# Chunked attention and two feed-forward layers on one core: weight conversion moved to the end of each attention tick with a fourth tile, v in another row order, relu squared from PSUM

## The chip, the cores and the metric

One core of a Trainium2 chip runs the whole program. The metric is device time in microseconds. The kernel before took 1264.05 us, the median of three runs (1263.99 to 1264.7).

## The reference

Attention is computed within chunks of 64 positions: 4 batches, 8 heads, 576 positions (9 chunks) and 64 numbers a head. Its output becomes x, 2304 tokens by 512, and goes through two layers.

```
scores = scale * (q_c @ k_c.T);  attn = softmax(scores);  x = attn @ v_c
h = max(x @ w_in, 0);            x = (h * h) @ w_out                    # 512 -> 2048 -> 512
for e in range(4): out += p[:, e] * (max(x @ w1[e], 0) @ w2[e])         # 512 -> 1024 -> 512
```

The first layer's weights arrive as 64-bit floats; q, k, v and the rest are 32-bit.

## The kernel before

**Ticks.** The order of all instructions is the order of the code; each engine works through its own list in that order and waits where an operand is missing. The first part runs in ticks r = 0, 1, 2, ... (the loop at L660). A tick of attention treats one tile of 128 positions (two chunks, all 8 heads), 18 tiles in all: `s1_stage(r)` makes the scores on TensorE and subtracts the row maximum on VectorE (two reduces L239 and two subtracts L240); `norm_stage(r-1)` divides by the row sums (L251 to L254, VectorE); `s2_stage(r-2)` transposes the weights (L260) and ScalarE copies them out (L262); `s0_stage(r+1)` transposes the next q and then the next k (L218, copies L222); `s3_stage(r-2)` multiplies by v (L274) and writes x as a rounded part (L281, ScalarE) and a rest (L282, VectorE); `exp_stage(r)` is ScalarE's exponential (L246). So `s3` stands on TensorE behind both transposes of tick r.

**First layer.** From tick 5 on, step m = r - 5 runs between these stages: `l1(m)` is one 128-row slice of x @ w_in for one block of tokens (384 or 512), 12 matmuls (L298), then relu (L308, ScalarE), the square (L309, VectorE), its rounded part (L311) and its rest (L312). `l2(m-1)` is 12 matmuls of the second product (L328), for the slice that the step before made. In a tick the first nine matmuls of `l1` come after `s1`, the last three after the q transpose, a quarter of `l2` (d = 0) before the k transpose, a quarter (d = 1) after it, then `s3`, and the last two quarters (d = 2, 3) at the tick's end.

**Weight units.** A unit is 128 rows or columns of w_in or w_out. Unit load (L108, L113) brings 512 KB into one of 4 `raw` tiles. `unit_convert` turns 64-bit into 32-bit in a `cv` tile: two operations on ScalarE (L125, L126), four on VectorE (L127, L130, L135, L138), two on GpSimd (L139, L140). `unit_split`, one tick or more later, makes a rounded part on ScalarE (L151) and a rest on GpSimd (L152), and so frees the `cv` tile. The first eight units are called u0 to u7 here, in the list `order`: w_in 0, w_in 1, w_out 0, w_in 2, w_out 1, w_in 3, w_out 2, w_out 3. They are converted in ticks 2, 3, 4, 4, 5, 6, 6, 7 (`FIRST`) and split at the end of the following tick, after that tick's conversions. `l1(m)` needs w_in m, from the start of tick 5 + m; `l2(m-1)` needs w_out m-1, from the middle of that tick. In the code before, L125 to L130 stand before the `s2` of a tick, and L135 to L140 before its `s3`.

**Loads.** SyncE issues the loads in the order of the code: in each tick first the weight units, then q and k of tile r + 2, and in some ticks v. A unit's load waits until a `raw` tile is free, and everything behind it on SyncE waits too. Eight semaphores tell of landed DMAs, taken in turn.

**PSUM.** From tick 5 on all the stages of attention share three banks ("t") in turn; `l1` has one bank ("h").

Of the kernel before, what the change touches and what calls it, by code (L numbers as in the profile page):

```python
# [10 lines left out]
F32 = mybir.dt.float32  # L11
F32R = mybir.dt.float32r
AF = mybir.ActivationFunctionType
ALU = mybir.AluOpType
# [4 lines left out]
P = 128  # L19
CH = 64  # L20
# [10 lines left out]
WARM = 8  # L31
SECOND = [-3, -2, -1, 1, 2, 3, 4, 5]
RAW_BUFS = 4
CV_BUFS = 3
HALF = 384
NSUP = 3
SWAP = 63
# [9 lines left out]
def tile_kernel(ctx, tc, q, k, v, moe_w_in, moe_w_out, moe2_p, moe2_w1, moe2_w2, out):  # L47
    nc = tc.nc
# [3 lines left out]
    E, _, F2 = moe2_w1.shape  # L52
    KD = DM // P
    HX = H // 2
    NTILE = NT // P
    NCB = S // CH
# [14 lines left out]
    staging = ExitStack()  # L71
    cvp = staging.enter_context(tc.tile_pool(name="cvp", bufs=CV_BUFS))
    rawp = staging.enter_context(tc.tile_pool(name="rawp", bufs=RAW_BUFS))
# [22 lines left out]
    def bank(tags):  # L96
        n = turn.get(tags, 0)
        turn[tags] = n + 1
        tag = tags[n % len(tags)]
        return ps.tile([P, 512], F32, tag=tag, name="ps" + tag, bufs=BUFS[tag])  # L100
# [58 lines left out]
    qkv, vt = {}, {}  # L159
    xh, xl = {}, {}  # L160
# [27 lines left out]
    def new_v(b):  # L188
        vt[b] = qkp.tile([P, HX, NCB, D], F32, tag="v", name="v")

    def load_v(b, c0, c1):
        if b not in vt:
            new_v(b)
        for h in range(H):
            j, x = divmod(h, 2)
            nc.sync.dma_start(
                out=vt[b][x * CH:(x + 1) * CH, j, c0:c1, :],
                in_=v[b, h, c0 * CH:c1 * CH, :].rearrange("(c k) d -> k c d", k=CH),
            )
            if h % 2:  # L200
                yield

    def load_v_chunk(b, c, engines):
        if b not in vt:
            new_v(b)
        for x in range(2):
            engines[x].dma_start(
                out=vt[b][x * CH:(x + 1) * CH, :, c, :],
                in_=v[b, x::2, c * CH:(c + 1) * CH, :].rearrange("j k d -> k j d"),
            )  # L210
            yield

# [12 lines left out]
    def s1_stage(t, tags):  # L225
        qt, kt = qT.pop(t), kT.pop(t)
        pt = [bank(tags)[:, :HX * CH].rearrange("p (j k) -> p j k", j=HX) for _ in range(2)]
        for c in range(2):
            cs = slice(c * CH, (c + 1) * CH)
            for j in range(HX):  # L230
                for x in range(2):
                    r = slice(x * CH, (x + 1) * CH)
                    nc.tensor.matmul(  # L233
                        pt[x][cs, j, :], lhsT=qt[r, j, cs], rhs=kt[r, j, cs], start=True, stop=True
                    )
        e = qkp.tile([P, HX, 2, CH], F32, tag="e", name="e", bufs=LAG_A + 1)
        mx = qkp.tile([P, 2, HX, 1], F32, tag="mx", name="mx")
        for x in range(2):
            nc.vector.tensor_reduce(out=mx[:, x], in_=pt[x], axis=AX.X, op=ALU.max)  # L239
            nc.vector.tensor_tensor(  # L240
                out=e[:, :, x, :], in0=pt[x], in1=mx[:, x].to_broadcast([P, HX, CH]), op=ALU.subtract
            )
        et[t] = e

    def exp_stage(t):
        nc.scalar.activation(out=et[t], in_=et[t], func=AF.Exp, scale=scale)  # L246
# [17 lines left out]

    def s3_stage(t, tags):
        a = aT.pop(t)
        pt = bank(tags).rearrange("p (j s) -> p j s", j=HX)
        for j in range(HX):
            for c in range(2):
                b, cc = divmod(2 * t + c, NCB)  # L270
                cs = slice(c * CH, (c + 1) * CH)
                for x in range(2):
                    r = slice(x * CH, (x + 1) * CH)
                    nc.tensor.matmul(  # L274
                        pt[r, j, cs], lhsT=vt[b][r, j, cc, :], rhs=a[r, j, cs], start=True, stop=True
                    )
        tb, off = block_of[t]
        if off == 0:
            new_x(tb)
        hi = xh[tb][:, :, off:off + P]  # L280
        nc.scalar.copy(hi, pt)  # L281
        nc.vector.tensor_tensor(  # L282
            out=xl[tb][:, :, off:off + P], in0=pt, in1=hi.bitcast(F32), op=ALU.subtract
        )


    steps = [(p, tb, f) for p in range(npass1) for tb in range(NB) for f in range(G)]
# [3 lines left out]
    def l1(i):  # L291
        p, tb, f = steps[i]
        T = BLOCKS[tb]
        ah, al = halves[p * G + f, 0]
        ph = bank("h" if "w" not in late else "httt")
        for kk in range(KD):
            for n, (w, x) in enumerate(((ah, xh), (ah, xl), (al, xh))):
                nc.tensor.matmul(  # L298
                    ph[:, :T], lhsT=w[:, kk, :], rhs=x[tb][:, kk, :],
                    start=(kk == 0 and n == 0), stop=(kk == KD - 1 and n == 2),  # L300
                )
            if kk < KD - 1:
                yield
        o = GP_AT + i % (LAG + 1) * 1024
        hi, lo = ar[:, o:o + 512], ar[:, o + 512:o + 1024]
        gh[i], gl[i] = hi, lo
        r = rp.tile([P, 512], F32, tag="r", name="r")
        nc.scalar.activation(out=r[:, :T], in_=ph[:, :T], func=AF.Relu)  # L308
        nc.vector.tensor_tensor(out=r[:, :T], in0=r[:, :T], in1=r[:, :T], op=ALU.mult)  # L309
        yield  # L310
        nc.scalar.copy(hi[:, :T], r[:, :T])  # L311
        nc.vector.tensor_tensor(  # L312
            out=lo[:, :T], in0=r[:, :T], in1=hi[:, :T].bitcast(F32), op=ALU.subtract
        )
# [46 lines left out]
    for sp in range(NSUP):  # L361
        if sp < NSUP - 1:
            r = [starts[2 * sp] + i * P for i in range(3)] + [starts[2 * sp + 1] + i * P for i in range(3)]
        else:
            r = [starts[NB - 1] + i * P for i in range(3)] + [starts[2 + i] + HALF for i in range(3)]
# [200 lines left out]
    def at(tick, kind, fn, *args):  # L566
        jobs[kind].setdefault(max(0, tick), []).append((fn, args))

    def do(tick, kind):
        return [fn(*args) for fn, args in jobs[kind].pop(tick, ())]  # L570

    for t in range(2, NTILE):
        at(t - 2, "load", load_qk, t, (nc.sync, nc.scalar if t == 2 else nc.sync))
    for b in range(B):
        if b == 0:
            for c in (2, 3):
# [22 lines left out]
    with tc.manual_schedule():  # L599
# [39 lines left out]
        def run(chunks, n=None):  # L639
            while n is None or n > 0:  # L640
                try:
                    next(chunks)
                except StopIteration:
                    return
                n = None if n is None else n - 1
# [13 lines left out]
        for r in range(LEAD + NS + LAG):  # L659
            m = r - LEAD  # L660
            tags = "ttthaaaa" if m < 0 else "t"
            ch = mlp(m) if m >= 0 else iter(())
            if r == NTILE + LAG_A:
                att.close()
                late["x"] = ctx.enter_context(tc.tile_pool(name="xq", bufs=1, side="right"))
                late["w"] = lw.enter_context(tc.tile_pool(name="wpb", bufs=RING_B, side="right"))
            merge(do(r, "load"))
            if r < NTILE + LAG_A:
                if r < NTILE:
                    s1_stage(r, tags)  # L670
                if 0 <= r - 1 < NTILE:
                    norm_stage(r - 1)
                conv = do(r, "convert")
                for c in conv:
                    next(c)
                run(ch, 3)
                if 0 <= r - LAG_A:
                    s2_stage(r - LAG_A, tags)
                if r + 1 < NTILE:
                    s0_stage(r + 1, tags, 0)  # L680
                run(ch, 2)
                if r + 1 < NTILE:
                    s0_stage(r + 1, tags, 1)
                for c in conv:
                    run(c)
                run(ch, 1)
                if 0 <= r - LAG_A:
                    s3_stage(r - LAG_A, tags)
                if r < NTILE:
                    exp_stage(r)  # L690
                do(r, "split")
            else:
                if r == SWAP:
                    staging.close()
                    late["raw"] = ctx.enter_context(tc.tile_pool(name="raw", bufs=1, reuse_waits="tile"))
                for fn, args in early.pop(r, ()):
                    fn(*args)
                if r > y0_at:
                    next(late.setdefault("y0", y_combine(0)), None)
                if m < NS:  # L700
                    run(ch, KD + 2)
                    conv = do(r, "convert")
                    for c in conv:
                        next(c)
                    run(ch, 1)
                    for c in conv:
                        run(c)
                    do(r, "split")
            if m < NS:
                run(ch)  # L710
# [68 lines left out]
```

## Time and profile before

| | |
|---|---|
| median of 3 runs | 1264.05 us |
| profiled execution, device time | 1261.85 us |
| its span, first to last instruction | 1260.1 us |
| TensorE matmul busy | 1231.7 us (98%), 7048 instructions |
| TensorE weight loads | 1090.4 us (87%) |
| VectorE | 705.0 us (56%), 1135 |
| ScalarE | 521.3 us (41%), 934 |
| GpSimd | 628.8 us (50%), 507 |
| granted TensorE clock, mean | 0.989 |

Busy shares are means over the span. The first part (attention and first layer, to about 500 us) and the second layer have different limits, so a share says little of a stage; the windows below cut it. Matmul busy time is modelled. In the profile PE is TensorE, PEld its weight loads, DVE VectorE, ACT ScalarE, POOL GpSimd, SP SyncE.

### The profile page before, as it was taken

To read this page: it belongs to the slowest core of one execution; us is meant where nothing else is said; L and a number is where in the kernel's file an instruction comes from. 1 tells how busy PE (TensorE), PEld (TensorE's weight loads), DVE (VectorE), ACT (ScalarE), POOL (GpSimd) and SP (SyncE) were. 2 spreads that over 40 slices of the span, in tenths; PEclk is the share of its full clock that TensorE was granted. 3 is DMA by queue.
4 is the path that set the end of the run, shared out by engine and by line. 5 is a ranking of instruction groups with operands and counts; after the bars stand their busy time and mean duration, and the time that the engine had idled before them with its cause. 6 is when DMAs were issued, how large, how long until landed. Compare 5 with 4: busy or idle time off the path is not lost.

```text
span 1260.1 us, 18090 instructions
## 1 busy us (share of the span) xinstructions
PE 1231.7 (98%) x7048; PEld 1090.4 (87%) x7048; DVE 705.0 (56%) x1135; ACT 521.3 (41%) x934; POOL 628.8 (50%) x507
## 2 busy tenths in 40 slices
PE   6799999999999999999999999999999999999998
PEld 5688788988988988888888888888888888888887
DVE  4876667755765355355555573555555735555555
ACT  3654455432432223633333355333333553333331
POOL 0530046431432022766776686767766866666650
PEclk7889999999999999999999999999999999999999
DMA  9947012210201000222222223222222232222211
GB/s 209 197 77 168 5 51 87 66 51 17 67 1 50 1 1 17 67 67 68 67 67 67 68 76 109 68 69 70 69 69 70 66 122 68 70 67 69 67 35 66
DMA packets 136838, 87.19 MB, mean 69 GB/s; under 512 B 62769, under 2 KB 120113, under 8 KB 136753
## 3 DMA queue, kind: packets, MB, share of 16 engines
q1 hardware_dynamic: 133088, 85.12, 24.9%
q10 hardware_dynamic: 3664, 0.92, 0.4%
q8 instruction: 55, 0.90, 0.3%
q14 instruction: 31, 0.25, 0.1%
HBM read 81.30 MB, written 4.72 MB: 68 GB/s over the span
## 4 chain that ended last, share of the span: by engine, by line
PE 91%; DVE 3%; ACT 1%; issue 0%; POOL 0%; DVEq 0%
PE psa L543 32%; PE pst L498 24%; PE psa L328 14%; PE pst L298 9%; PE psh L298 6%; PE psh L498 4%; PE pst L274 1%; PE pst L233 1%; PE pst L218 1%; DVE cv L127 0%; PE pst L260 0%; DVE r L309 0%; DVE cv L130 0%; DVE ar L312 0%; DVE cv L135 0%
## 5 line engine op out<-in xcount | busy, mean ns | idle before, releaser
L543 PE MATMUL psa<-ar 128*128 128x512 f32 x1728 | 445.7, 393 | 0.0
L543 PEld LDWEIGHTS psa<-ar 128*128 128x128 f32 x1728 | 320.0, 188 | 50.3
L466 POOL TENSOR_TENSOR ar<-raw,ar 128x896 fp32r<-128x896 f32 x96 | 204.2, 2129 | 274.4 <-ACT ar L465 274.4
L498 PE MATMUL pst<-ar 128*128 128x384 f32 x1728 | 339.2, 335 | 0.9 <-ACT u L507 0.9
L498 PEld LDWEIGHTS pst<-ar 128*128 128x128 f32 x1728 | 307.3, 188 | 22.8 <-ACT u L507 1.6
L556 DVE SCALAR_TENSOR_TENSOR o<-psa,prob,o 128x512 f32<-128x512 f32 x270 | 201.5, 747 | 173.4 <-PE psa L543 173.4
L139 POOL TENSOR_TENSOR raw<-raw 128x512 f32<-128x512 f32 x32 | 36.2, 1131 | 230.0 <-DVE raw L138 97.6
L456 POOL TENSOR_TENSOR raw<-raw 128x256 f32<-128x256 f32 x192 | 141.3, 754 | 8.8 <-DMA raw<-in_moe_w 5.2
L475 POOL TENSOR_TENSOR ar<-raw,ar 128x512 fp32r<-128x512 f32 x96 | 123.4, 1306 | 12.5 <-ACT ar L474 12.5
L309 DVE TENSOR_TENSOR r<-r 128x512 f32<-128x512 f32 (+1 forms) x80 | 64.9, 811 | 108.9 <-ACT r L308 108.8
L328 PE MATMUL psa<-ar 128*128 128x512 f32 (+1 forms) x480 | 114.7, 379 | 1.3 <-POOL ar L152 1.2
L507 ACT COPY u<-pst 128x384 f32<-128x384 f32 x96 | 46.0, 479 | 163.8 <-PE pst L498 163.8
L511 ACT ACTIVATE ar<-pst 128x384 fp32r<-128x384 f32 x96 | 47.2, 492 | 149.7 <-DVE pst L532 116.3
L328 PEld LDWEIGHTS psa<-ar 128*128 128x128 f32 x480 | 87.6, 191 | 14.3 <-POOL ar L152 1.5
L328 PE MATMUL psa<-ar,h 128*128 128x512 f32 (+1 forms) x320 | 93.7, 373 | 1.6 <-ACT ar L311 0.8
L511 ACT ACTIVATE ar<-psh 128x384 fp32r<-128x384 f32 x96 | 47.2, 492 | 109.8 <-DVE psh L521 78.6
L465 ACT CAST ar<-raw 128x896 fp32r<-128x896 f32 x96 | 90.1, 939 | 0.0
L312 DVE TENSOR_TENSOR ar<-r,ar 128x512 fp32r<-128x512 f32 (+1 forms) x80 | 61.6, 770 | 39.9 <-ACT ar L311 39.1
L512 DVE SCALAR_TENSOR_TENSOR ar<-psh,ar 128x384 fp32r<-128x384 f32 x96 | 53.5, 558 | 53.6 <-ACT ar L511 53.6
L311 ACT CAST ar<-r 128x512 fp32r<-128x512 f32 (+1 forms) x80 | 46.1, 577 | 71.0 <-DVE r L309 71.0
L512 DVE SCALAR_TENSOR_TENSOR ar<-pst,ar 128x384 fp32r<-128x384 f32 x96 | 53.5, 557 | 31.2 <-ACT ar L511 29.1
L298 PE MATMUL pst<-ar,h 128*128 128x512 f32 (+1 forms) x240 | 69.3, 370 | 0.0
(106 smaller groups left out, 1482.9 us busy)
## 6 DMA issues: line engine op xcount, KB each, us to landing
raw<-in_moe_w SPq DMA_DIRECT2D x48, 512.0 KB, 3.9
raw<-in_moe_w SPq DMA_DIRECT2D x48, 256.0 KB, 3.0
raw<-in_moe_w SPq DMA_DIRECT2D x96, 128.0 KB, 3.0
raw<-in_moe_w_in SPq DMA_DIRECT2D x16, 512.0 KB, 3.8
raw<-in_moe_w_out SPq DMA_DIRECT2D x16, 512.0 KB, 3.7
out<-o SPq DMA_DIRECT2D x18, 256.0 KB, 3.2
q<-in_q SPq DMA_DIRECT2D x16, 256.0 KB, 4.7
v<-in_v SPq DMA_DIRECT2D x24, 144.0 KB, 4.5
```

The source lines that it names most:

```text
L298: nc.tensor.matmul(ph[:, :T], lhsT=w[:, kk, :], rhs=x[tb][:, kk, :], start=(kk == 0 and n == 0), stop=(kk == KD - 1 and n == 2),)
L309: nc.vector.tensor_tensor(out=r[:, :T], in0=r[:, :T], in1=r[:, :T], op=ALU.mult)
L328: nc.tensor.matmul(o, lhsT=w, rhs=y, start=(f == 0 and n == 0), stop=(f == G - 1 and n == 2))
L456: nc.gpsimd.tensor_tensor(out=r[:, o], in0=r[:, a], in1=r[:, b], op=op)
L465: nc.scalar.copy(h, a)
L466: nc.gpsimd.tensor_tensor(out=l, in0=a, in1=h.bitcast(F32), op=ALU.subtract)
L475: nc.gpsimd.tensor_tensor(out=l, in0=a, in1=h.bitcast(F32), op=ALU.subtract)
L498: nc.tensor.matmul(p, lhsT=w[:, kk, :], rhs=y[:, kk, :], start=(kk == 0 and z == 0 and u in (0, 1, 3)), stop=(kk == 1 and z == 2 and u in ...
L511: nc.scalar.activation(out=h, in_=p, func=AF.Relu)
L512: nc.vector.scalar_tensor_tensor(out=l, in0=p, scalar=0.0, in1=h.bitcast(F32), op0=ALU.max, op1=ALU.subtract)
L543: nc.tensor.matmul(p, lhsT=w[:, ts], rhs=y[:, i, :], start=(i == 0 and z == 0), stop=(i == 1 and z == 2))
L556: nc.vector.scalar_tensor_tensor(out=o, in0=p, scalar=pe, in1=o, op0=ALU.mult, op1=ALU.add)
```

## The change

Four things change. `unit_convert` runs whole at the end of a tick of attention, after `exp_stage` and before the splits, with four `cv` tiles for three. The v tile holds, for odd j, the two heads of a pair in swapped row halves; `s1` writes the scores in that order, and `s3` runs the 32 matmuls one column half after the other, with alternating row halves, into two PSUM banks, which are read by two L281 and two L282 operations of half the size. The first chunks of v are loaded by four DMAs of 32 KB for two of 64 KB. The square becomes max(PSUM, 0) times the relu, and k of tile 2 is loaded from SyncE's queue, no longer from ScalarE's.

```diff
-CV_BUFS = 3
+CV_BUFS = 4
 def load_v(b, c0, c1):
             j, x = divmod(h, 2)
+            x ^= j % 2
 def load_v_chunk(b, c, engines):
-        for x in range(2):
+        vb = v[b].rearrange("(jj z) s d -> z s jj d", jj=2)
+        for z, x in ((0, 0), (1, 1), (3, 0), (2, 1)):
             engines[x].dma_start(
-                out=vt[b][x * CH:(x + 1) * CH, :, c, :],
-                in_=v[b, x::2, c * CH:(c + 1) * CH, :].rearrange("j k d -> k j d"),
+                out=vt[b][x * CH:(x + 1) * CH, z // 2::2, c, :], in_=vb[z, c * CH:(c + 1) * CH],
             )
 def s1_stage(t, tags):
             nc.vector.tensor_tensor(
-                out=e[:, :, x, :], in0=pt[x], in1=mx[:, x].to_broadcast([P, HX, CH]), op=ALU.subtract
+                out=e.rearrange("p (jj jb) x k -> p jj (jb x) k", jb=2)[:, :, slice(1, 3) if x else slice(0, 4, 3), :],
+                ...
 def s3_stage(t, tags):
-        pt = bank(tags).rearrange("p (j s) -> p j s", j=HX)
-        for j in range(HX):
-            for c in range(2):
-                ...
-                for x in range(2):
-                    r = slice(x * CH, (x + 1) * CH)
-                    nc.tensor.matmul(pt[r, j, cs], lhsT=vt[b][r, j, cc, :], rhs=a[r, j, cs], ...)
+        pt = [bank(tags)[:, :2 * P].rearrange("p (j s) -> p j s", j=2) for _ in range(2)]
+        for x in (1, 0):
+            for jj in range(HX // 2):
+                for c in range(2):
+                    ...
+                    for jb in range(2):
+                        j = 2 * jj + jb
+                        r = slice((x ^ jb) * CH, (x ^ jb) * CH + CH)
+                        nc.tensor.matmul(pt[jb][x * CH:(x + 1) * CH, jj, cs], lhsT=vt[b][r, j, cc, :], rhs=a[r, j, cs], ...)
-        nc.scalar.copy(hi, pt)
-        nc.vector.tensor_tensor(out=xl[tb][:, :, off:off + P], in0=pt, ...)
+        for jb in range(2):
+            hi = xh[tb][:, jb::2, off:off + P]
+            nc.scalar.copy(hi, pt[jb])
+            nc.vector.tensor_tensor(out=xl[tb][:, jb::2, off:off + P], in0=pt[jb], ...)
 def l1(i):
-        nc.vector.tensor_tensor(out=r[:, :T], in0=r[:, :T], in1=r[:, :T], op=ALU.mult)
+        nc.vector.scalar_tensor_tensor(out=r[:, :T], in0=ph[:, :T], scalar=0.0, in1=r[:, :T], op0=ALU.max, op1=ALU.mult)
-        at(t - 2, "load", load_qk, t, (nc.sync, nc.scalar if t == 2 else nc.sync))
+        at(t - 2, "load", load_qk, t)
 # the loop over ticks, r < NTILE + LAG_A
-                conv = do(r, "convert")
-                for c in conv:
-                    next(c)
                 run(ch, 3)
                 ...
-                for c in conv:
-                    run(c)
                 run(ch, 1)
                 ...  # s3_stage, exp_stage
+                for c in do(r, "convert"):
+                    run(c)
                 do(r, "split")
```

## Rows read from the trace of the kernel before

**Rows 1.** Windows: busy us and instructions of each engine; granted clock, DMA share.

```profile
20.00:40.00 20.00, 12.82 (x222) 11.37 (x224) 17.60 (x41) 11.83 (x22) 6.25 (x6) 0.84 1.08 205
40.00:60.00 20.00, 15.59 (x175) 13.91 (x172) 17.46 (x34) 11.99 (x24) 11.03 (x9) 0.85 0.87 198
80.00:100.00 20.00, 20.00 (x260) 18.03 (x257) 13.32 (x28) 10.91 (x22) 1.28 (x1) 1.00 0.33 76
```

**Rows 2.** Chain that ended last, 0 to 180 us: start, length, what.

```profile
74.94 1.49 PE psh L298 x7
...
93.82 0.54 PE psa L328 x3
94.36 0.44 PE pst L218 x4
...
95.32 1.08 PE pst L274 x32
96.40 1.27 PE psa L328 x6
97.67 0.91 PE pst L233 x30
```

**Rows 3.** Waits, 0 to 100 us: total, times, longest.

```profile
ACT cv L125 <- POOL ar L152: 14.4, 4, 6.1
```

**Rows 4.** Timeline of POOL, 17 to 76 us: start, length, operation.

```profile
52.85 2.84 POOL L152 TENSOR_TENSOR ar<-cv,ar 128x512 fp32r<-128x512 f32 x2
...
65.55 1.27 POOL L152 TENSOR_TENSOR ar<-cv,ar 128x512 fp32r<-128x512 f32 x1
71.23 1.04 POOL L139 TENSOR_TENSOR raw<-raw 128x512 f32<-128x512 f32 x1 [4.41 <-issue]
...
73.60 2.85 POOL L152 TENSOR_TENSOR ar<-cv,ar 128x512 fp32r<-128x512 f32 x2
```

**Rows 5.** Timeline of ACT, the same stretch.

```profile
39.30 0.59 ACT L281 CAST ar<-psh 128x512 fp32r<-128x512 f32 x1 [0.51 <-PE psh L274]
39.78 0.63 ACT L246 ACTIVATE e<-e 128x512 f32<-128x512 f32 x1
...
66.85 0.67 ACT L125 ACTIVATE cv<-raw 128x512 f32<-128x512 f32 x1 [6.12 <-POOL ar L152]
```

**Rows 6.** Timeline of PE, from 19 to 75 us.

```profile
37.51 0.65 PE L218 MATMUL pst<-ident,k 128*128 128x128 f32 x4 [3.44 <-DMA k<-in_k]
```

**Rows 7.** Timeline of DVE, 17 to 76 us.

```profile
36.81 0.42 DVE L127 TENSOR_SCALAR cv<-cv 128x512 f32<-128x512 f32 x1
...
40.19 1.15 DVE L138 TENSOR_SCALAR raw<-cv 128x512 int32<-128x512 int32 x1
...
41.85 0.41 DVE L239 TENSOR_REDUCE mx<-pst 128x4 f32<-128x256 f32 x1
...
43.09 0.42 DVE L240 TENSOR_TENSOR e<-pst,mx 128x256 f32<-128x256 f32 x1
```

**Rows 8.** Waits of SyncE's DMA queue, 0 to 80 us.

```profile
SPq L113 <- POOL cv L140: 3.6, 2, 2.5
...
SPq L108 <- DMA k<-in_k: 1.8, 1, 1.8
```

**Rows 9.** Timeline of all engines, 0 to 45 us.

```profile
4.60 1.28 ACT L222 ACT_TABLE_LOAD   x1 [4.60 <-issue]
...
7.99 2.58 SPq L207 DMA_DIRECT2D v<-in_v  x4
...
11.27 0.58 ACT L222 COPY qT<-psa 128x512 f32<-128x512 f32 x1 [4.30 <-DMA raw<-in_moe_w_in]
...
16.41 1.09 PE L218 MATMUL pst<-ident,k 128*128 128x128 f32 x4 [1.35 <-DMA k<-in_k]
```

**Rows 10.** The page's costliest groups: count, busy us, mean ns.

```profile
L309 DVE TENSOR_TENSOR r<-r 128x512 f32<-128x512 f32 (+1 forms) x80 | 64.9, 811 | 108.9 <-ACT r L308 108.8
...
L512 DVE SCALAR_TENSOR_TENSOR ar<-pst,ar 128x384 fp32r<-128x384 f32 x96 | 53.5, 557 | 31.2 <-ACT ar L511 29.1
```

More of the change, by code (lines that the diff above doesn't have):

```diff
@@ L240, in s1_stage @@
             nc.vector.tensor_tensor(
-                out=e[:, :, x, :], in0=pt[x], in1=mx[:, x].to_broadcast([P, HX, CH]), op=ALU.subtract
+                out=e.rearrange("p (jj jb) x k -> p jj (jb x) k", jb=2)[:, :, slice(1, 3) if x else slice(0, 4, 3), :],
+                in0=pt[x].rearrange("p (jj jb) k -> p jj jb k", jb=2),
+                in1=mx[:, x].to_broadcast([P, HX, CH]).rearrange("p (jj jb) k -> p jj jb k", jb=2),
+                op=ALU.subtract,
             )
@@ L266, in s3_stage @@
         a = aT.pop(t)
-        pt = bank(tags).rearrange("p (j s) -> p j s", j=HX)
-        for j in range(HX):
-            for c in range(2):
-                b, cc = divmod(2 * t + c, NCB)
-                cs = slice(c * CH, (c + 1) * CH)
-                for x in range(2):
-                    r = slice(x * CH, (x + 1) * CH)
-                    nc.tensor.matmul(
-                        pt[r, j, cs], lhsT=vt[b][r, j, cc, :], rhs=a[r, j, cs], start=True, stop=True
-                    )
+        pt = [bank(tags)[:, :2 * P].rearrange("p (j s) -> p j s", j=2) for _ in range(2)]
+        for x in (1, 0):
+            for jj in range(HX // 2):
+                for c in range(2):
+                    b, cc = divmod(2 * t + c, NCB)
+                    cs = slice(c * CH, (c + 1) * CH)
+                    for jb in range(2):
+                        j = 2 * jj + jb
+                        r = slice((x ^ jb) * CH, (x ^ jb) * CH + CH)
+                        nc.tensor.matmul(
+                            pt[jb][x * CH:(x + 1) * CH, jj, cs],
+                            lhsT=vt[b][r, j, cc, :],
+                            rhs=a[r, j, cs],
+                            start=True,
+                            stop=True,
+                        )
         tb, off = block_of[t]
@@ L279, in s3_stage @@
             new_x(tb)
-        hi = xh[tb][:, :, off:off + P]
-        nc.scalar.copy(hi, pt)
-        nc.vector.tensor_tensor(
-            out=xl[tb][:, :, off:off + P], in0=pt, in1=hi.bitcast(F32), op=ALU.subtract
-        )
+        for jb in range(2):
+            hi = xh[tb][:, jb::2, off:off + P]
+            nc.scalar.copy(hi, pt[jb])
+            nc.vector.tensor_tensor(
+                out=xl[tb][:, jb::2, off:off + P], in0=pt[jb], in1=hi.bitcast(F32), op=ALU.subtract
+            )
     steps = [(p, tb, f) for p in range(npass1) for tb in range(NB) for f in range(G)]
@@ L308, in l1 @@
         nc.scalar.activation(out=r[:, :T], in_=ph[:, :T], func=AF.Relu)
-        nc.vector.tensor_tensor(out=r[:, :T], in0=r[:, :T], in1=r[:, :T], op=ALU.mult)
+        nc.vector.scalar_tensor_tensor(
+            out=r[:, :T], in0=ph[:, :T], scalar=0.0, in1=r[:, :T], op0=ALU.max, op1=ALU.mult
+        )
         yield
```

## The prediction

> **What bounds the kernel now.** I cut the span into windows first. From 80 us on TensorE is busy all the time at full clock; in 40 to 60 us it has 15.59 of 20 us at a mean clock of 0.85, while VectorE is at 17.46 and the DMA engines at 0.87 [rows 1]. So there are two stages. After 75 us TensorE's list is the time, and only what shortens that list counts. Before, a chain through several engines is the time, and the change works there. The chain of waits names the border: the first matmuls of l1(3), the fourth step, at 74.94 us, directly behind GpSimd's split of u5 [rows 2, 4]; from there it lies on TensorE. I therefore look for two numbers: when l1(3) can start, and what a later tick costs.
>
> The list of waits gives the early stage's pattern. ScalarE's L125 waited 14.4 us in four waits for a `cv` tile [rows 3]. The longest wait for a `cv` tile, 6.12 us, ended at 66.85, when the split of u4 was through [rows 4, 5]. TensorE waited 3.44 us for k of tile 5, until 37.51 [rows 6]; VectorE spent just that time, from 36.81 to 41.34, on the conversion of u2 and u3 [rows 7]. That cover is what the change gives up.
>
> **Later ticks: the product with v.** Now 32 matmuls of s3 take 1.08 us, and the 32 of s1, which already alternate row halves inside one column half and write two banks, take 0.91 [rows 2]. New s3 has the order of s1, so I take 0.91: 0.17 less. The bounds are 0 and, if the pairs gain twice that, 0.34. From tick 8 to 19 there are 12: **-2.0 us** (0 to -4.1). By the Trainium skill, page "TensorE: Matmul & The Clock Gate", section "Wait — 56ns, not 53.3ns?", matmuls never start closer than about 25 ns; 32 of them would be 0.80 us, and the term -3.4 by that estimate. The row for s1 is 28 ns each and decides.
>
> What goes with it: the second L281 and L282. Whole, L281 takes 0.59 and the next operation starts 0.48 later [rows 5]; two halves are some 0.8 on ScalarE. On VectorE the half of L282 is like the subtract of the scores, 256 columns from PSUM, 0.42 [rows 7]. The three banks now serve seven tiles a tick, so the second score bank of the next tick waits for the first half of L282, about 0.1 + 0.4 + 0.45 = 0.95 us after s3. TensorE has 1.27 us of l2 there first [rows 2], which covers it; if VectorE were busy then, it would be up to 0.4 us a tick. The subtract's new output pattern has the same elements: 0.
>
> **Relu squared.** L309 averages 811 ns over blocks of 384 and 512 columns, 461 in the mean of the five blocks; the like operation with a PSUM operand takes 557 for 384 [rows 10], so 668 for 461. VectorE may gain 0.14 us a step, beside a TensorE that is busy throughout and a VectorE that is not [rows 1]: 0 on the path (-1 to +0.5, as single waits fall). PSUM bank "h" is held 0.6 us longer, but the next l1 is most of a tick away.
>
> **The start.** The ninth load waits for k's landing, 1.8 us [rows 8], though it writes another tile: no more than eight loads are out at once. The second v chunk's four small loads are now numbers 9 to 12 (before, the first nine ended with u0's load). ScalarE issues one of these and can do so only when the second k has landed, about 7.99 [rows 9]; with the table load of 1.28 behind it, its first copy moves from 5.9 to about 9.9, and s1(0) by 4 us. Most of this is absorbed: now ScalarE's second pair of copies waits 4.30 us, until 11.27, for a load's landing because k of tile 2 stands in its queue, and TensorE then waits for that k until 16.41 [rows 9]. On SyncE's queue this k goes out at about the same time and ScalarE is free. Net effect on s1(2): 0 (-1.5 to +2). But SyncE has more issues, 0.65 us each (2.58 for 4) [rows 9], and u0's load, now number 13, waits for the fifth, an estimated 3 us more; what follows is late by 1.5 to 2.5 us.
>
> On top of this, u4's load in tick 3 waits for u0's `raw` tile. Now this costs SyncE up to 2.5 us [rows 8]; u0's conversion moves behind the products, L281 and the exponential of tick 2, some 2 us, and q and k of tile 5 stand behind that load. The two delays overlap, since the DMA engines catch up when issues are late. k of tile 5: **+1.6 us** (0 to +3.0).
>
> **Conversion at the tick's end.** On ScalarE it passes the copies of aT, q and k, the relu, L281 and the exponential; on VectorE the square and L282; GpSimd's order stays. Waiting behind it now: L151, L311 and L312, and the next tick's score maxima, without which the next q and k have no bank. The work of the eight units is the same.
>
> Take tick 4 with k of tile 5 as now. Transpose done 38.1; s3 1.08: 39.2; two L281 0.8: 40.0; exponential 0.63: 40.6; L125 0.67: 41.3. VectorE's two conversions took 4.53 [rows 7]: 45.8. Only then come the maxima of s1(5), 1.66 [rows 7]: 47.5. k's transpose and s3 of tick 5, 1.5: 49.0; L281, exponential, L125, 2.1: 51.1; one conversion 2.25: 53.3; GpSimd's two operations 2.37 (71.23 to 73.60), then the split of u2, 1.27 [rows 4]: 57.0. Now this split ends at 54.2 (half of the two from 52.85): **+2.8 us**.
>
> From here it is a loop, because l2's first quarter waits for the split, and s3 stands behind l2, and the conversion now behind s3: quarter, k, quarter, s3 = 0.54 + 0.44 + 0.54 + 0.91 = 2.43 [rows 2]; L281 to L125 2.1; VectorE 2.25; GpSimd 2.37; split 1.27: 10.4 for a tick with one unit. With two, GpSimd's second 2.37 adds up and VectorE's second lies beside it: 12.8. Split of u2 to split of u4 (tick 6, u5 and u6) takes 12.6 now, to 66.82; u4 to u5 (tick 7, u7) 8.1, to 74.9 [rows 4]. So **+0.2** and **+2.3 us** (0 to +4 together; more if VectorE's operations stretch beside GpSimd's, as L138 to 1.15 [rows 7]). The fourth `cv` tile removes the waits of rows 3, but what is late next is this loop.
>
> l1(3) needs u5 and stands at the start of tick 8: 74.9 + 1.6 + 2.8 + 0.2 + 2.3 = 81.8, **+6.9 us**. All else of tick 8 is early by then, and from there TensorE runs through.
>
> In ticks 17 to 19, conversions of the next units push L312 behind them: it ends about 5.0 us after s3, where l2 asks for it after 4.8 to 5.1: +0.5 in all (0 to +1.5).
>
> **Sum.** +6.9 - 2.0 + 0 + 0.5 = +5.4 us on the profiled execution's 1261.85, of which 1260.1 is span: 1267.25. That execution was 2.2 us under the median of the runs, so the median would be 1269.5.
>
> **Rivals.** *A, the cv wait was the price (faster).* If the weights arrive early enough from the tick's end, ticks 5 to 7 run at VectorE's work. With 13.3 us per 20 in two and a half plain ticks [rows 1], a tick has 5.4 us of it, and a unit adds 2.25: 7.7, 9.9 and 7.7, together 25 us, where now 33 us lie between the maxima of s1(5) and l1(3) [rows 2, 7]. So -8 - 2 = -10: 1254. For it: the 14.4 us of waits [rows 3]. Against: those waits ended with splits that l2 awaited just as much. It decides if the split of u5 ends before about 75 us.
>
> *B, gain and loss cancel (no change).* k of tile 5 comes no later, and the conversion of u7 begins early enough that the loop's last turn takes 8 to 9 us: +2.8 + 0 + 0.5 - 2.0: 1265, within 2.5 us of before.
>
> *C, the start costs more.* With eight loads out at once and half of them 32 KB, the DMA engines run dry before 16 us, and k of tile 5 comes 5 us late where I took 1.6: 1273. For it: DMA share of 1.08 in 20 to 40 us, so lost DMA time isn't regained [rows 1]. In the Trainium skill, "DMA: Bandwidth & Descriptors", section "Measured (HBM→SBUF, 128 partitions, SWDGE, issued from GpSimd)", transfers under 64 KB are called descriptor-dominated; that would be this rival, but here the 64 KB already come in rows of 64 numbers of 4 bytes, and the small loads have the same rows.
>
> *D, the row order does nothing.* s3 stays at 1.08: 1271.5, inside the forecast's own range.
>
> **Chances.** Forecast with D 0.52, own range 1266.6 to 1272.5; A 0.16; B 0.18; C 0.14. A run of this kernel can tell some 0.2% or 2.5 us. Faster 0.16, same 0.18, slower 0.66. The bounds of the terms reach from about 1264 to 1277; below that only A is left, and 1261 to 1275 leaves out most of it and the upper end, together less than 0.2.
>
> **What would show it.** s3 at 0.91 us in the chain of waits, and later ticks 0.17 shorter. No wait of L125 for L152. Split of u2 after 57 us, of u5 after 80, and TensorE idle some 5 us in front of l1(3). k of tile 5 landing after 38.5. Wrong would be an l1(3) before 76 us, or a stretch after 90 us that changes by more than 2 us otherwise than through s3.

## The result, and the profile after

The changed kernel takes 1277.49 us, the median of 4 runs (1274.75 to 1279.83), where the kernel before takes 1264.22 on the same chip: a ratio of 1.0106, with a 95% interval of 1.0093 to 1.0119. It is 13.3 us slower. The forecast was 1269.5, and its range ended at 1275.

The profiled execution has a span of 1275.7 us, 15.6 more than before. l1(3), the border between the stage bound by a chain and the stage bound by TensorE, starts at 91.54 us for 74.94 [rows 2]: 16.6 later. What follows it takes 1184.2 us for 1185.2. So the whole loss lies ahead of l1(3). (Of the kernel before the profile shows an execution 2.2 us under its median, so the profiled spans lie 15.6 us apart and the medians 13.3.) In the code after, the lines that matter are L219 (transposes), L234 (`s1`), L281 (`s3`), L293 and L294 (the halves of the old L281 and L282), L310 (`l1`), L321 (the square), L325 and L326 (its parts) and L342 (`l2`); L125 to L152 are as before.

Windows of the kernel after, with the columns of rows 1:

```profile
0.00:20.00 20.00, 12.45 (x133) 11.11 (x135) 4.80 (x12) 5.76 (x9) 0.69 (x6) 0.74 0.81 173
...
40.00:60.00 20.00, 13.68 (x162) 12.13 (x163) 17.86 (x35) 10.38 (x21) 9.81 (x9) 0.67 0.90 175
60.00:80.00 20.00, 13.88 (x119) 11.80 (x118) 14.24 (x27) 8.26 (x16) 10.57 (x9) 0.76 0.88 141
80.00:100.00 20.00, 14.84 (x144) 13.12 (x144) 8.44 (x19) 7.16 (x16) 5.46 (x4) 0.74 0.16 36
```

Two more windows of the kernel before:

```profile
0.00:20.00 20.00, 12.28 (x137) 10.60 (x138) 4.94 (x13) 6.77 (x11) 0.68 (x6) 0.79 1.06 204
...
60.00:80.00 20.00, 17.62 (x186) 15.16 (x184) 15.33 (x28) 8.40 (x17) 11.72 (x9) 0.83 0.66 113
```

In 40 to 60 us the mean granted clock is 0.67 where it was 0.85, and in 80 to 100, which the loop now reaches, it is 0.74 where it was 1.00 [rows 1]. Busy time of TensorE hides this: in 60 to 80 us its 13.88 us hold 119 matmuls, 117 ns each in the mean, where 17.62 us held 186, 95 ns each, though not quite of the same mix.

The chain that ended last, of the kernel after: start, length, what. This is the last turn of the loop, from the split of u4 to l1(3), and then a late tick.

```profile
78.35 1.25 POOL ar L152
...
79.65 0.69 PE psa L342
80.34 0.85 PE pst L219 x4
81.19 0.96 PE psa L342 x3
82.15 1.53 PE pst L281 x32
...
84.83 0.55 ACT cv L125
85.39 0.56 ACT raw L126
85.95 1.03 ACT ar L151 x2
...
87.63 1.26 POOL raw L139
88.96 1.28 POOL cv L140
90.24 1.26 POOL ar L152
...
91.54 2.61 PE psh L310 x7
...
106.42 0.91 PE pst L281 x30
```

The turn has the members that the prediction named, in their order; beside VectorE's conversion, which ends at 87.50, the chain names ScalarE's operations, which end 0.1 us earlier. But TensorE's part of it takes 4.03 us (0.69, 0.85, 0.96, 1.53) where 2.43 were summed, and l1's seven matmuls take 2.61 for 1.49 [rows 2]. At 106.42 the new `s3` takes 0.91 us, for 1.08 (the chain merges 30 of its 32 matmuls, as it does for `s1`).

Waits of the kernel after, 0 to 110 us: total, times, longest. None of L125 for L152 is left (14.4 us in [rows 3]); TensorE now waits for L152, 7.5 us in two waits.

```profile
PE psh L310 <- POOL ar L152: 4.4, 1, 4.4
...
PE psa L342 <- POOL ar L152: 3.1, 1, 3.1
```

Timeline of GpSimd, the kernel after: start, length, operation.

```profile
62.72 1.72 POOL L152 TENSOR_TENSOR ar<-cv,ar 128x512 fp32r<-128x512 f32 x1
72.08 1.09 POOL L139 TENSOR_TENSOR raw<-raw 128x512 f32<-128x512 f32 x1 [7.64 <-ACT ar L151]
73.25 1.36 POOL L140 TENSOR_TENSOR cv<-cv,raw 128x512 f32<-128x512 f32 x1
75.76 1.23 POOL L139 TENSOR_TENSOR raw<-raw 128x512 f32<-128x512 f32 x1 [1.15 <-issue]
...
78.31 1.29 POOL L152 TENSOR_TENSOR ar<-cv,ar 128x512 fp32r<-128x512 f32 x1
```

The first row is the split of u3; that of u2 ends just as it starts, at 62.76 us. In the kernel before it ended at 54.44, by the chain of waits:

```profile
52.89 1.55 POOL ar L152
```

The split of u4 ends at 79.60, for 66.82 [rows 4]. Between two turns GpSimd stands idle for 7.64 us.

Timeline of VectorE in the same conversions, those of u5 and u6, and the end of that of u7:

```profile
70.33 0.43 DVE L130 TENSOR_SCALAR cv<-cv 128x512 int32<-128x512 int32 x1
70.79 0.69 DVE L135 SCALAR_TENSOR_TENSOR cv<-raw,cv 128x512 int32<-128x512 int32 x1
...
72.31 1.15 DVE L130 TENSOR_SCALAR cv<-cv 128x512 int32<-128x512 int32 x1
73.49 1.67 DVE L135 SCALAR_TENSOR_TENSOR cv<-raw,cv 128x512 int32<-128x512 int32 x1
...
87.07 0.43 DVE L138 TENSOR_SCALAR raw<-cv 128x512 int32<-128x512 int32 x1
```

The second unit's L130 and L135 run beside GpSimd's L139 and L140 and take 1.15 and 1.67 us for 0.43 and 0.69; each ends 0.3 to 0.6 us after GpSimd's operation has ended. GpSimd then waits 1.15 us for this second unit, until 75.76.

Timeline of TensorE, the kernel after:

```profile
41.18 1.09 PE L219 MATMUL psa<-ident,k 128*128 128x128 f32 x4 [3.30 <-DMA k<-in_k]
...
53.00 1.61 PE L281 MATMUL pst<-aT,v 64*64 64x64 f32 x32
...
58.06 3.25 PE L310 MATMUL psh<-ar 128*128 128x384 f32 x9
...
64.77 1.16 PE L342 MATMUL psa<-ar 128*128 128x384 f32 x3
...
67.09 0.97 PE L281 MATMUL pst<-aT,v 64*64 64x64 f32 x32
...
70.17 1.85 PE L310 MATMUL psh<-ar 128*128 128x384 f32 x9
```

k of tile 5 is transposed at 41.18 us, 3.7 later than before [rows 6]. `s3` takes 1.61 and nine matmuls of `l1` 3.25 up to 62 us; a little later the same groups take 0.97 and 1.85 in this view. The quarter of l2 that needs u2 starts at 64.77, 2.0 us after the split of u2, because TensorE is still at the work ahead of it until then.

The load of k of tile 5 on SyncE's queue, before:

```profile
30.18 1.36 SPq L184 DMA_DIRECT2D k<-in_k  x1
```

and after:

```profile
33.41 1.69 SPq L184 DMA_DIRECT2D k<-in_k  x1
```

### The profile page after: what moved, and what is told of

The parts are those of the page before. It is cut to its first block, busy times and chain, and to the rows that moved or that the text cites. A ratio compares the mean times of both kernels' runs of the same rounds, so it can differ in the third digit from the quotient of the medians.

```text
span 1275.7 us, 18149 instructions
## 1 busy us (share of the span) xinstructions
PE 1234.8 (97%) x7048; PEld 1092.9 (86%) x7048; DVE 691.0 (54%) x1153; ACT 524.1 (41%) x952; POOL 623.3 (49%) x507
## 4 chain that ended last, share of the span: by engine, by line
PE 91%; DVE 1%; ACT 1%; POOL 0%; issue 0%; DVEq 0%
PE psa L557 31%; PE pst L512 23%; PE psa L342 15%; PE pst L310 9%; PE psh L310 6%; PE psh L512 4%; PE pst L281 1%; PE pst L219 1%; PE pst L234 1%; PE pst L265 0%; DVE cv L130 0%; ACT ar L325 0%; DVE r L321 0%; POOL ar L152 0%; DVE cv L127 0%
## 5 line engine op out<-in xcount | busy, mean ns | idle before, releaser
L139 POOL TENSOR_TENSOR raw<-raw 128x512 f32<-128x512 f32 x32 | 35.0, 1095 | 257.3 <-issue 105.2
L342 PE MATMUL psa<-ar 128*128 128x512 f32 (+1 forms) x480 | 114.6, 378 | 4.9 <-POOL ar L152 3.1
L342 PEld LDWEIGHTS psa<-ar 128*128 128x128 f32 x480 | 87.5, 191 | 17.9 <-POOL ar L152 3.3
L342 PE MATMUL psa<-ar,h 128*128 128x512 f32 (+1 forms) x320 | 93.2, 372 | 1.1 <-ACT ar L325 0.8
L326 DVE TENSOR_TENSOR ar<-r,ar 128x512 fp32r<-128x512 f32 (+1 forms) x80 | 57.9, 723 | 39.5 <-ACT ar L325 37.9
L310 PE MATMUL psh<-ar 128*128 128x512 f32 (+1 forms) x264 | 66.8, 394 | 5.2 <-POOL ar L152 4.4
L310 PE MATMUL pst<-ar,h 128*128 128x512 f32 (+1 forms) x240 | 69.3, 370 | 0.0
L321 DVE SCALAR_TENSOR_TENSOR r<-pst,r 128x512 f32<-128x512 f32 (+1 forms) x48 | 30.7, 640 | 71.2 <-ACT r L320 71.2
```

Of the source, the lines that this page charges most:

```text
L310: nc.tensor.matmul(ph[:, :T], lhsT=w[:, kk, :], rhs=x[tb][:, kk, :], start=(kk == 0 and n == 0), stop=(kk == KD - 1 and n == 2),)
L326: nc.vector.tensor_tensor(out=lo[:, :T], in0=r[:, :T], in1=hi[:, :T].bitcast(F32), op=ALU.subtract)
L342: nc.tensor.matmul(o, lhsT=w, rhs=y, start=(f == 0 and n == 0), stop=(f == G - 1 and n == 2))
```

## The experiments

Each was timed in three rounds beside the kernel before; a ratio is to that kernel, with its 95% interval.

**The change with the conversion in its old places** (row order, square, small loads, k of tile 2 and four `cv` tiles stay).

```diff
+                conv = do(r, "convert")
+                for c in conv:
+                    next(c)
                 run(ch, 3)
...
+                for c in conv:
+                    run(c)
                 run(ch, 1)
...
-                for c in do(r, "convert"):
-                    run(c)
```

> The changed kernel with the conversion back in its two old places of the tick (still four cv tiles). Loop theory (the conversion's place behind s3 makes the early ticks a serial loop of conversion, split, l2, s3): the loop is gone, only the later loads stay; l1(3) starts at 73 to 78 us (changed kernel 91.5, before 74.9), time 1262 to 1266 us. Loads theory (the small v loads and k of tile 2 on SyncE's queue delay everything): k of tile 5 still lands after 40 us, l1(3) after 83, time 1272 or more.

1259.86 us, ratio 0.997 (0.9958 to 0.9983). Chain of waits:

```profile
75.08 1.54 POOL ar L152
...
76.67 1.49 PE psh L310 x7
```

l1(3) starts 14.9 us earlier than after and at full clock. The place of the conversion alone costs 17.6 us, more than the whole loss; the other parts, the fourth `cv` tile among them, together gain 4.3, more than was expected of them.

**The conversion at the tick's end alone, with four `cv` tiles, in the kernel before** (the lines above, the other way round).

```diff
-CV_BUFS = 3
+CV_BUFS = 4
...
-                conv = do(r, "convert")
...
+                for c in do(r, "convert"):
+                    run(c)
```

> The kernel before with the conversion moved to the tick's end and four cv tiles, nothing else. Loop theory: most of the loss is here; l1(3) at 83 to 88 us, k of tile 5 about 2 us late because u4's load waits longer for its raw tile, time 1273 to 1278 us (no gain of s3). Loads theory: l1(3) before 78, time 1264 to 1267.

1277.95 us, ratio 1.0114 (1.0098 to 1.013): as slow as the whole change. l1(3) came later than the 83 to 88 us that were expected, and k of tile 5, at 39.93, 2.4 us later than before [rows 6]. Chain of waits:

```profile
90.19 2.61 PE psh L298 x7
```

**The change with the splits ahead of the conversions.**

```diff
+                do(r, "split")
                 for c in do(r, "convert"):
                     run(c)
-                do(r, "split")
```

> The changed kernel with each tick's splits ahead of its conversions, so that no split stands behind a conversion on ScalarE or GpSimd. Loop theory: each turn loses L125, VectorE's 2 us and GpSimd's 2.4 us; the split of u5 ends 7 to 13 us earlier than 91.5, l1(3) at 78 to 84 us, time 1264 to 1270 us. Loads theory: no more than 2 us less than the changed kernel's 1277.5.

1269.17 us, ratio 1.0041 (1.0025 to 1.0057). Chain of waits:

```profile
82.28 0.91 PE pst L234 x30
83.18 1.81 PE psh L310 x9
```

The splits no longer stand behind the next conversions on ScalarE and GpSimd, and 8.3 us come back (l1(3) starts 8.4 us earlier than after); a little under half of the price of the place is the turn through the split.

**Four loads of 32 KB for the first v chunks, alone.**

```diff
-        for x in range(2):
+        vb = v[b].rearrange("(jj z) s d -> z s jj d", jj=2)
+        for z, x in ((0, 0), (1, 1), (2, 0), (3, 1)):
```

> The kernel before with each load of a v chunk made by four 32 KB DMAs for two of 64 KB, nothing else (k of tile 2 still on ScalarE's queue). Loop theory: the first copies of ScalarE some 4 us later, of which 1 to 3 us are left at l1(3): 1265 to 1267 us. Loads theory: the greater part of the 13 us, 1271 us or more.

1268.02 us, ratio 1.0031 (1.0021 to 1.004). Timeline of TensorE:

```profile
41.01 0.99 PE L218 MATMUL pst<-ident,k 128*128 128x128 f32 x4 [2.06 <-DMA k<-in_k]
```

The small loads alone make k of tile 5 3.5 us later [rows 6] and cost 3.9 us, between what the two theories gave. Its load is issued at 32.39 us, for 30.18 before: 2.2 of the 3.5 lie in SyncE's queue, which has more loads to issue ahead of it.

**The row order alone** (v in pairs, the scores' order, the new `s3` with its two halves; the small loads come with it), in the kernel before.

```diff
+            x ^= j % 2
...
+        for z, x in ((0, 0), (1, 1), (3, 0), (2, 1)):
...
+        pt = [bank(tags)[:, :2 * P].rearrange("p (j s) -> p j s", j=2) for _ in range(2)]
+        for x in (1, 0):
+            for jj in range(HX // 2):
```

> The kernel before with the row order of v alone: the swapped rows, the new s3 with two banks and two halves of L281 and L282, and the four small loads a chunk that it needs; conversion, cv tiles, square and k of tile 2 as before. The small loads alone cost 3.9 us (e4). Loop theory: s3 at 0.91 for 1.08 in 12 ticks gives 2.0 to 2.3 back: 1265 to 1267 us. If the early ticks feel the second bank (a wait of s1 for L282's first half): 1268 or more.

1265.17 us, ratio 1.0008 (0.9998 to 1.0017). Against the small loads alone this is 2.8 us less, in which `s3`, 0.17 shorter in 12 ticks, has 2.0.

**Four `cv` tiles alone.**

```diff
-CV_BUFS = 3
+CV_BUFS = 4
```

> The kernel before with a fourth cv tile alone. If the 14.4 us of waits of L125 for a cv tile were a price: l1(3) 3 to 8 us earlier than 74.9, time 1256 to 1261. If they ended with splits that l2 awaited as well: 1262 to 1264.5.

1260.69 us, ratio 0.9965 (0.9953 to 0.9977). Its waits, 0 to 100 us:

```profile
ACT cv L125 <- POOL ar L152: 1.1, 1, 1.1
```

l1(3) starts at 72.69 us, 2.25 earlier, where 3 to 8 were expected. The waits of rows 3 did have a price. Against this kernel the conversion at the tick's end costs 17.3 us, the second measure of the same step.

**The square with one PSUM operand alone** (L309).

```diff
-        nc.vector.tensor_tensor(out=r[:, :T], in0=r[:, :T], in1=r[:, :T], op=ALU.mult)
+        nc.vector.scalar_tensor_tensor(
+            out=r[:, :T], in0=ph[:, :T], scalar=0.0, in1=r[:, :T], op0=ALU.max, op1=ALU.mult
+        )
```

> The kernel before with the square made from one PSUM operand alone. VectorE is off the path in most places: 1262.5 to 1265 us. If VectorE's operations beside GpSimd's set the stretch from 191 to 218 us and the early ticks, and the PSUM operand is spared the stretching: 1260 to 1262.

1262.16 us, ratio 0.9982 (0.9972 to 0.9992): 1.9 us gained where nothing was forecast. The square's durations (least, median and longest in ns, first and last start), in the kernel before:

```profile
L309 DVE TENSOR_TENSOR r<-r x80: 546/691/1779, 48.7 to 499.2; 128x512 f32<-128x512 f32 x48, 128x384 f32<-128x384 f32 x32
```

and in this kernel:

```profile
L309 DVE SCALAR_TENSOR_TENSOR r<-pst,r x48: 543/690/692, 181.9 to 492.6; 128x512 f32<-128x512 f32 x30, 128x384 f32<-128x384 f32 x18
L309 DVE SCALAR_TENSOR_TENSOR r<-psh,r x32: 549/687/692, 48.8 to 498.1; 128x512 f32<-128x512 f32 x18, 128x384 f32<-128x384 f32 x14
```

The median is the same; what goes are the long ones, up to 1779 ns. One of these in the kernel before, and GpSimd's operation beside it:

```profile
272.93 1.73 DVE L309 TENSOR_TENSOR r<-r 128x512 f32<-128x512 f32 x1 [1.39 <-ACT r L308]
```

```profile
272.79 1.32 POOL L140 TENSOR_TENSOR cv<-cv,raw 128x512 f32<-128x512 f32 x1
```

The new operation's name is not the reason: L135 has the same name, both its inputs in SBUF, and takes 1.67 us beside GpSimd. Between 240 and 510 us VectorE's busy time falls from 149.06 to 136.28. l1(3) starts no earlier (75.31); behind it the profiled execution takes 1183.6 us for 1185.2. Where there the 1.6 us came from isn't settled: TensorE's idle time in 200 to 220 us is 1.13 for 1.63.

**k of tile 2 on SyncE's queue alone.**

```diff
-        at(t - 2, "load", load_qk, t, (nc.sync, nc.scalar if t == 2 else nc.sync))
+        at(t - 2, "load", load_qk, t)
```

> The kernel before with k of tile 2 issued by SyncE alone. ScalarE's copies no longer wait 4.30 us; s1(1) starts 2 to 2.7 us earlier than 12.4. If that wait was on the path: 1261 to 1263 us. If loads set the pace until tick 5 anyway: 1263.5 to 1265.

1265.12 us, ratio 1.0005 (0.9996 to 1.0015): no difference that can be told.

**The change with zero products in TensorE's waits.** Matmuls of a zero tile fill TensorE's waits in ticks 5 to 8, in banks where they are overwritten or add nothing.

```diff
+    def fill(o, n, new=False):
+        z, y = late["fill"]
+        for _ in range(n):
+            nc.tensor.matmul(o[:, :P], lhsT=z, rhs=y, start=new, stop=new, skip_group_check=True)
...
+        fill(ph, {2: 2, 3: 12}.get(i, 0), True)
...
+                fill(pacc[d], {0: 3, 1: 10}.get(i, 0), i == 0)
...
+                if m == 0:
+                    fill(bank("a"), 6, True)
```

> The changed kernel with matmuls of a zero tile (their products are overwritten or add zero) put ahead of TensorE's waits in ticks 5 to 8: 3 before l2(0), 10 before l2(1), 2 before l1(2), 12 before l1(3), 11 in tick 5. Nothing else changes. Clock theory (TensorE falls to 1.2 GHz in the waits, so that the loop's own matmuls take twice the time): the granted clock of 60 to 100 us rises from 0.75 to over 0.9, the turn from the split of u4 to that of u5 falls from 11.9 to 10.5 us, l1(3) starts at 86 to 89.5 us for 91.5 and its first tick is 2 us shorter; time 1270 to 1274 us. If the clock adds nothing: l1(3) at 91 or later, 1277 or more.

1272.79 us, ratio 1.0068 (1.0053 to 1.0083): 4.7 us less than the change, with 76 matmuls more. Windows, as above:

```profile
60.00:80.00 20.00, 16.09 (x154) 13.88 (x153) 15.99 (x31) 8.75 (x17) 11.67 (x9) 0.96 0.81 155
80.00:100.00 20.00, 17.53 (x214) 15.75 (x214) 11.29 (x24) 8.52 (x19) 6.76 (x5) 0.96 0.18 40
```

The chain of waits of the same kernel, in the last turn:

```profile
80.14 1.59 PE pst L281 x32
...
89.60 1.49 PE psh L316 x7
```

The clock of both windows is 0.96, for 0.76 and 0.74. k of tile 5 came 1.2 us later here than after (42.41), so everything up to the split of u2 is late by as much (64.03), but the turn from u2 to u4 took 13.9 us (to 77.92) for 16.8. In that turn `s3`, in the timeline of TensorE:

```profile
65.42 0.97 PE L281 MATMUL pst<-aT,v 64*64 64x64 f32 x32
```

From the split of u2 to the end of `s3` it took 2.4 us for 5.3; from there to the split of u4 11.5 us in both kernels. So the gain of this turn is TensorE's alone. In the next turn the clock had fallen again (`s3` 1.59), and it stayed long, 11.7 us for 11.9. Behind l1(3) the rest took 1181.6 us for 1184.2.

**Kernels that the experiments point to.** Four `cv` tiles and the square in the kernel before:

```diff
-CV_BUFS = 3
+CV_BUFS = 4
...
-        nc.vector.tensor_tensor(out=r[:, :T], in0=r[:, :T], in1=r[:, :T], op=ALU.mult)
+        nc.vector.scalar_tensor_tensor(
...
```

> The kernel before with the fourth cv tile and the square from PSUM only. Alone these gave 3.4 and 1.9 us; if they add up: 1258 to 1259.5 us.

1259.75 us, ratio 0.9966 (0.9954 to 0.9979): 4.6 us less than before by the medians, where four tiles alone give 3.4 and the square 1.9; by the ratios no more than four tiles alone (0.9965). Whether the two gains add isn't settled.

The change with the conversion in its old places, k of tile 2 back on ScalarE, and v chunks 2 to 8 in eight loads of 112 KB for the small ones and those behind them:

```diff
-            for c in (2, 3):
-                at(0, "load", load_v_chunk, b, c, (nc.sync, nc.sync))
-            at(1, "load", load_v, b, 4, NCB)
+            at(0, "load", load_v, b, 2, NCB)
```

> The changed kernel with the conversion in its old places, k of tile 2 on ScalarE's queue, and v of chunks 2 to 8 by eight loads of 112 KB for eight small and eight of 80 KB. With the small loads' cost (3.9 us for both pairs of chunks) halved, k's 1.0 us gone and the row order's gain kept: 1256 to 1258.5 us. If the first two chunks' small loads are all of the cost: 1259 to 1261.

1257.56 us, ratio 0.9949 (0.9934 to 0.9964). Its first window:

```profile
0.00:20.00 20.00, 11.52 (x139) 10.12 (x140) 5.24 (x14) 6.86 (x11) 0.68 (x6) 0.83 1.01 177
```

and its chain of waits:

```profile
72.44 1.54 POOL ar L152
74.03 1.49 PE psh L310 x7
```

The DMA engines are busy for 1.01 of the first 20 us, for 0.81 in the kernel after, and k of tile 5 is transposed at 37.82 (its load is issued at 30.44). This kernel beats both.

The same with the splits ahead of the first half of the conversions:

```diff
+                do(r, "split")
                 conv = do(r, "convert")
...
-                do(r, "split")
```

> c2_order_merged with each tick's splits ahead of the first half of its conversions. Loop theory: the splits of u4 and u5 no longer stand behind a conversion on GpSimd, l1(3) 2 to 4 us earlier: 1253 to 1256 us. If ScalarE's L151 now waits for GpSimd at the tick's start and holds up the copies: 1258 or more.

1257.35 us, ratio 0.9946 (0.9932 to 0.9961). TensorE no longer waits for a split at l1(3) and runs from 73.69 us on, but that is where the kernel just above had come anyway: the expected gain isn't there.

## Why the prediction failed

Each step had the sign that was forecast, and each sign that it listed to look for was there: `s3` at 0.91, no wait of L125 for L152, the split of u2 after 57, of u5 after 80, an idle TensorE ahead of l1(3), k of tile 5 after 38.5. One of its signs of being wrong was there too: the first tick behind l1(3) grew by some 2.6 us otherwise than through `s3`. What failed is one step's size, that of the loop: "From here it is a loop ... 10.4 for a tick with one unit ... With two ... 12.8", and the path into it. The terms ahead of l1(3), by the kernel after:

| term | forecast, us | measured, us |
|---|---|---|
| k of tile 5 | +1.6 | +3.7 |
| from there to the split of u2 | +2.8 | +4.6 |
| turn u2 to u4 | +0.2 (12.8 long) | +4.5 (16.8 long) |
| turn u4 to u5 | +2.3 (10.4 long) | +3.8 (11.9 long, to l1(3)) |
| l1(3) | +6.9 | +16.6 |

The forecast had the split of u2 before end at 54.2, half of two; the chain has 54.44. Of the 9.7 us that are missing, k of tile 5 has 2.1, TensorE's part of the two turns 4.5 and VectorE's stretching in ticks 4 and 6 2.4, by the traces; the rest is spread.

- **The loop was summed at TensorE's full clock.** 2.43 us for its part came from rows of a stretch in which TensorE never waits. In a loop with one work item at a time it does wait, and the granted clock falls to a mean of 0.67 to 0.76, so its groups run partly at the lower level, 1.2 GHz: 4.03 us in the last turn, and 5.3 in the turn before it, in which `l1`, too, was late. The run with zero products shows it as a cause: at 0.96 that turn was 13.9 us, 1.1 over the forecast for it, with 2.4 us for TensorE's part. 4.7 us of the time came back; in the profiled executions 1.9 ahead of l1(3) and 2.6 behind it, in the first tick, which is outside the loop. The Trainium skill, page "TensorE: Matmul & The Clock Gate", section "HAM oscillation — how this bites in real kernels", tells of such a loop, there with waits for DMA between the groups of matmuls: each group starts at the lower clock again, and half of the time spent at that clock is lost. The trace agrees in kind, with 3.25 us for nine matmuls that take 1.85 at 70.17.
- **VectorE's conversion was taken as undisturbed.** Two units take 5.8 us at the tick's end, in tick 4 as in tick 6, where 4.53 was summed, since the second unit's L130 and L135 now meet GpSimd's work for the first; the sum also let GpSimd's second conversion follow its first at once, and it waits 1.15 us. In the old places, with the change's other parts, the pair of tick 4 takes 4.52 and only L138 is stretched: there VectorE does both units' L127 and L130 before GpSimd may begin. The prediction named this in brackets, from L138's 1.15 us [rows 7], and put no number on it. The Trainium skill, page "SBUF — State Buffer", section "Who interferes with whom", has the rule: of a VectorE operation that needs the shared port pair (two inputs in SBUF, or a two-port mode) and one of GpSimd, the later one waits until the other is through. The trace agrees, L130 at 1.15 and L135 at 1.67 us, and so do the squares: longest 1779 ns with two inputs in SBUF, 692 with one in PSUM.
- **Both make the loop's price a loss of overlap.** Before the change the conversions of a tick ran beside its products and transposes; put behind them, they stand in one row with them. (The prediction misread one row of this: TensorE's wait for k ended at 37.51, so the conversion from 36.81 to 41.34 lay for the most part beside k's transposes, `s3` and `s1`, not beside the wait.) By two pairs of kernels this costs 17.6 and 17.3 us (with four `cv` tiles on both sides), for the 5.3 of the forecast.
- **k of tile 5** was 3.7 us late, where 1.6 was taken and 5 was rival C's. The small loads alone make it +3.5 and the conversion's place alone +2.4: the two delays overlap, as forecast, but each is larger than their sum was taken to be. C's sign is there, a DMA share in the first 20 us of 0.81 for 1.06 before and 1.01 with merged loads. But most of the delay, 3.2 of the 3.7 us, lies in SyncE's queue, which issues this load at 33.41 for 30.18: the prediction's own two terms there, more issues and a wait for a `raw` tile, sized too small. What makes the rest, the loads' number or their size, isn't settled.
- **Rival A** was half right. The waits for a `cv` tile cost 3.4 us, which the forecast had at nothing because the loop's work was late anyway. But its point, the split of u5 before 75 us, was missed by some 17.
- **Rival B** fell with the same turn: forecast at 8 to 9 us, measured 11.9. **Rival D** fell: `s3` went from 1.08 to 0.91, as forecast.
- **The square** was taken from medians and means as a gain off the path; alone it took 1.9 us off, 0.9 beyond the bound of -1.
- **What comes behind l1(3)** changed by -1.0 us: -2.0 for `s3` as forecast, about +2.6 for the first tick at the lower clock, and about -1.6 for the rest, for which the square is the likely cause (alone it took 1.6 off here). That the sum is near the -1.5 of the forecast is luck: two terms that it did not have nearly cancel. The +0.5 for L312 isn't seen by itself.

By single edits, the conversion with four tiles +13.8, small loads +3.9, row order -2.8, square -1.9 and k of tile 2 +1.0 add up to +14.0, for the 13.3 measured. Each of them can be off by 1 us or so, so this does not show that the parts act apart: at k of tile 5 two of them overlap. But one of them is the whole loss.

The range failed with the sum. Its upper end took each term's own bound but let the terms share one condition, a full clock; when that is gone, all of them that hold TensorE's work grow together.

## What to carry to other kernels

Before moving work out of the shade of another engine, write down the loop that then closes and price each member under the conditions inside that loop: matmuls at the clock that a waiting TensorE is granted, and VectorE beside the GpSimd operation that it feeds. A wait that a larger buffer removes is worth trying alone first: here that one line gained 3.4 us, and the rearrangement around it lost 17. Splitting early loads into smaller ones, for a better layout, can cost more at the start than the layout gains in the steady part (here +3.9 for -2.8 us); with the same layout in larger loads both are to be had.

## What the runs showed of the hardware

- Matmuls that compute nothing made a program faster: 76 more of them took 4.7 us off, with a granted clock of 0.96 in 60 to 100 us for 0.74 to 0.76.
- 32 matmuls of 64 by 64 took 0.91 us with row halves alternating inside one column half and two PSUM banks, 1.08 with row and column half both changing at every matmul and one bank; the same work, with the same operand sizes. Whether the order or the second bank does it wasn't tried apart.
- The time of one VectorE operation of 512 columns went from 0.69 to 1.78 us by what GpSimd did beside it, and not at all when one of its inputs came from PSUM.
